# Who sums the two row halves at a group's end: ScalarE copies one half, VectorE adds the other from PSUM, and the swap is issued there

## The chip, the cores and the metric

The kernel runs on one core of a Trainium2 chip. Its time is that of the device, in microseconds (us), for one execution. Three executions were timed and one more was profiled.

## The reference

Two blocks follow each other. The first is an attention with polynomial features, and its output, turned into a matrix x of 4352 rows and 128 columns, is the input of the second. The second routes each row over eight experts with weights that are balanced by eight rounds of row and column normalisation, and adds up the experts' outputs:

```python
def _moe_ref(x, w_gate, w1, w2):
    logits = x @ w_gate
    logits = logits - logits.max()
    P = np.exp(logits)
    for _ in range(8):
        P /= P.sum(1, keepdims=True) + 1e-09
        P /= P.sum(0, keepdims=True) + 1e-09
        P *= N / E
    out = np.zeros((N, D), dtype=np.float32)
    for e in range(E):
        h = np.maximum(x @ w1[e], 0.0)
        ye = h @ w2[e]
        out += P[:, e:e + 1] * ye
    return out.astype(np.float32)
```

w1 has the shape 8 x 128 x 1024, w2 the shape 8 x 1024 x 128, all in float32.

## The kernel before

The attention, the routing weights and a part of the experts' work fill the first 197 us of the profiled execution. The rest is the function `weighted()`, in which the change lies.

**Groups, items, passes.** The rows of x are split into ten groups (`wgroups`). Groups 0 to 4 have 2 x 256 rows, groups 5 to 9 have 2 x 224 (n = 256 and n = 224). Each group goes through its list of experts; a pair of a group and an expert is an item, and each item is done in two halves of the hidden layer (s = 0 and s = 1). One half of an item is called a pass here. There are 120 of them, numbered 0 to 119 in the order of the list `todo`. Groups 1 to 8 multiply with seven products of half size in place of eight (a Strassen form); groups 0 and 9 (`whole`) use eight in the second layer.

**The order inside a pass.** Two generators take turns step by step. `firsts(t)` makes pass t's hidden layer: in each of its seven steps TensorE runs four 64 x 64 tiles in a form of two matmul records each (line 986) into the PSUM tiles `pair`, and ScalarE and VectorE turn them into h and ts (ScalarE: copies of lines 1061, 1067, 1070 and the relu of 993; VectorE: the additions of line 990, then lines 1086, 1092, 1093, 1094). `seconds(t - 1)` multiplies the pass before it with w2 (line 1120) and sums up in four PSUM banks, `acc[g][rho][q]`: rho tells the lower from the upper 64 rows of the array, q the two column halves of the result. So the last products of a group run in the first pass of the next group. That pass is called the closing pass; in the pass behind it the next group's first products are written into the same four banks, and in `into` the lower rows' products stand ahead of the upper rows' in each step. All engines take their instructions in the order in which the program issues them, which is written out by hand here.

**The end of a group.** When a bank pair q is complete, `ended(g, q)` has ScalarE copy the lower and the upper rows' sums to the tile `z` (line 1163): q = 0 in the closing pass's fourth step, q = 1 in its last (group 0 has only one pair, which is complete at the very end). The sum over rho, and for the seven-product form nine further additions, are not issued at once. They are put in the list `leisure`, and taken from it one by one at fixed places in later passes: `spare` gives them to VectorE, twice in each pass with s = 0, and `aside` to GpSimd, once in most passes. An entry None uses up a place and does nothing. The nine additions need the other 64 partitions' values, which a swap of two DMAs puts into the tile `w` (line 1192, SP's queue); it is issued along with the second sum over rho, and three entries None follow it. Then the result is added to `kept`, transposed and stored (`put`, lines 1214 and 681). `z`, `y` and `w` each exist once, so the next group's copy to z waits for the last reader of the old one.

In the last group (`LAST`) more places are taken: two at the start of its second passes and two at each `spare`. What is still left is issued on VectorE ahead of the last additions (`finish_last`, line 1235).

**SP's queue.** SP issues nearly all DMAs in the program's order: the stores; the weights of the next item, first layer at the start of a pass with s = 0 (line 851), second layer at the start of one with s = 1 (lines 860 and 862, w and ws); the routing weights (line 893); the swap of the inputs xf (line 904). Each waits in place until its buffer is free or its data is ready.

Of the kernel before, what the change touches and what calls it, by code (L numbers as in the profile page):

```python
# [10 lines left out]
F32 = mybir.dt.float32  # L11
U32 = mybir.dt.uint32
Act = mybir.ActivationFunctionType
Alu = mybir.AluOpType
# [36 lines left out]
def kernel(  # L51
# [12 lines left out]
    nc = tc.nc  # L64
    P = nc.NUM_PARTITIONS
# [887 lines left out]
    def weighted():  # L953
# [2 lines left out]
        pairs = [fps.tile([P, 2, 512], F32, name=f"pair{i}") for i in range(2)]  # L956
        copies = late[0].tile([P, 2, 3, 2 * NW], F32, name="copies", bufs=1)
        leisure, chores = [], []
        acc, counts = {}, {}
        todo = [(i, s) for i in range(len(witems)) for s in range(2)]  # L960

        def flat(t, n):
            return t.rearrange("p (r n) -> p r n", r=2)
# [6 lines left out]
        def firsts(t):  # L970
# [113 lines left out]
                relu(h[:, 3], h[:, 3])  # L1084
            else:
                nc.vector.scalar_tensor_tensor(ts[:, 0], h[:, 3], 0.0, h[:, 0], op0=Alu.max, op1=Alu.subtract)  # L1086
            spare(0)
            yield
            product(pa, 3, 7, False, True)
            relu(flat(h[:, 1], n), pa)  # L1090
            if g not in whole:
                nc.vector.tensor_tensor(ts[:, 2], h[:, 1], ts[:, 0], op=Alu.subtract)  # L1092
                nc.vector.scalar_tensor_tensor(ts[:, 1], h[:, 3], 0.0, h[:, 1], op0=Alu.max, op1=Alu.subtract)
                nc.vector.tensor_tensor(ts[:, 3], h[:, 2], ts[:, 2], op=Alu.subtract)  # L1094
            spare(1)
            yield

        def seconds(t):

            i, s = todo[t]  # L1100
            g, e = witems[i]
            lo, n, es = wgroups[g]
            _, w2, ws = forms[i]
            h, ts = rooms(t)
            if g not in acc:
                acc[g] = [[mps.tile([P, 512], F32, tag=f"s{2 * rho + q}", name="s") for q in range(2)]
                          for rho in range(2)]

            def raw(dh, k, r):
                return w2[:, 4 * r + 2 * k + s, H2 * dh:H2 * (dh + 1)]  # L1110

            def form(m, r):
                return ws[:, m, 2 * r + s]

            def into(half, w, x, r, q, place):
                per = 2 * len(es) * (4 if g == LAST else 8 if g == 0 else 3 if q else 4)
                for rho in range(2):
                    rows = slice(H2 * rho, H2 * (rho + 1))
                    c = counts[g, rho, q, half] = counts.get((g, rho, q, half), 0) + 1
                    yield lambda rho=rho, rows=rows, c=c: nc.tensor.matmul(  # L1120
                        acc[g][rho][q][H2 * half:H2 * (half + 1), n * place:n * (place + 1)], w[rows],
                        flat(x, n)[rows, r], start=c == 1, stop=c == per, tile_position=(H2 * rho, H2 * half))

            def both(x, y):
                for one, two_ in zip(x, y):
                    one()
                    two_()

            last = t + 1 == len(todo) or witems[todo[t + 1][0]][0] != g
            if g in whole:  # L1130
                for m, (k, u, b) in enumerate(((0, 0, 0), (1, 0, 2), (0, 1, 3), (1, 1, 1))):
                    for r in range(2):
                        q = u if g == LAST else 0
                        both(into(0, raw(0, k, r), h[:, b], r, q, u), into(1, raw(1, k, r), h[:, b], r, q, u))
                        if last and m == 3 and r == 1 and g == 0:
                            ended(g, 0)
                            finish_direct(g)
                        if last and m % 2 and r == 1 and g == LAST:
                            finish_last(g, u)
                        yield  # L1140
                return
            for m, (x, y) in enumerate((((raw, (0, 0), h[:, 0], 0, 0), (raw, (0, 1), h[:, 2], 0, 0)),
                                        ((form, (3,), h[:, 1], 0, 1), (form, (0,), ts[:, 0], 0, 1)),
                                        ((form, (2,), ts[:, 1], 1, 0), (form, (1,), ts[:, 2], 1, 0)))):
                for r in range(2):
                    both(into(0, x[0](*x[1], r), x[2], r, *x[3:]), into(1, y[0](*y[1], r), y[2], r, *y[3:]))
                    if last and m == 1 and r == 1:
                        ended(g, 0)
                    yield
            both(into(0, raw(1, 1, 0), ts[:, 3], 0, 1, 1), into(1, raw(1, 1, 1), ts[:, 3], 1, 1, 1))  # L1150
            if last:
                ended(g, 1)
                finish_seven(g)
            yield

        ends = {}

        def ended(g, q):
            n = wgroups[g][1]
            if g not in ends:  # L1160
                ends[g] = late[0].tile([P, 2, 2, 2 * NW], F32, tag="z", name="z", bufs=1)
            for rho in range(2):
                nc.scalar.copy(ends[g][:, rho, q, 0:2 * n], acc[g][rho][q][:, 0:2 * n])  # L1163

        def settle(g):
            while chores and chores[0][0] <= g:
# [3 lines left out]
        def plus(out_, x, y):  # L1170
            leisure.append((lambda engine: engine.tensor_tensor(out_, x, y, op=Alu.add), True))

        def finish_direct(g):
            settle(g)
            n = wgroups[g][1]
            z = ends[g]
            y = late[0].tile([P, 2, NW], F32, tag="y", name="y", bufs=1)[:, :, 0:n]
            plus(y, flat(z[:, 0, 0, 0:2 * n], n), flat(z[:, 1, 0, 0:2 * n], n))
            out_of(g, y)

        def finish_seven(g):
            settle(g)
            n = wgroups[g][1]
            z = ends[g]
            y = late[0].tile([P, 2, NW], F32, tag="y", name="y", bufs=1)[:, :, 0:n]
            w = late[0].tile([P, 2, 2 * NW], F32, tag="w", name="w", bufs=1)
            for q in range(2):
                plus(z[:, 0, q, 0:2 * n], z[:, 0, q, 0:2 * n], z[:, 1, q, 0:2 * n])

            def swap():  # L1190
                for s in range(2):
                    nc.sync.dma_start(out=w[H2 * (1 - s):H2 * (2 - s), :, 0:2 * n],
                                      in_=z[H2 * s:H2 * (s + 1), 0, :, 0:2 * n])

            last_sum = leisure.pop()[0]
            leisure.append((lambda engine: (last_sum(engine), swap()), True))
            leisure.extend([None] * 3)
            v, x = ([[u[:, q, n * a:n * (a + 1)] for a in range(2)] for q in range(2)] for u in (z[:, 0], w))
            t1, t2, t3 = (z[:, 1, 0, 0:n], z[:, 1, 0, n:2 * n], z[:, 1, 1, 0:n])
            lo_, up = lower, upper  # L1200
            plus(y[lo_, 0], v[0][0][lo_], x[0][0][lo_])
            plus(t1[lo_], v[0][0][lo_], x[1][0][lo_])
            plus(t1[up], x[0][0][up], v[1][0][up])
            plus(t2[lo_], x[0][1][lo_], v[0][1][lo_])
            plus(t1[up], t1[up], x[1][0][up])
            plus(y[lo_, 1], t1[lo_], t2[lo_])
            plus(t3[up], v[1][1][up], x[1][1][up])
            plus(y[up, 1], t1[up], v[0][1][up])
            plus(y[up, 0], t1[up], t3[up])
            out_of(g, y)  # L1210
# [154 lines left out]
```

## Time and profile before

| | |
|---|---|
| median of three runs | 916.24 us |
| lowest and highest | 915.18 and 918.57 us |
| profiled execution | 916.32 us |
| span of that execution | 914.5 us |
| mean granted clock of TensorE | 0.996 |
| busy: TensorE, VectorE, ScalarE, GpSimd | 98%, 79%, 61%, 28% |

The span runs from the first to the last instruction; the profiled execution's own time is 1.8 us longer. Busy TensorE time is modelled from pipelined matmuls, so 98% doesn't say that nothing is lost: how much a stretch loses is better read from the distance between the same step of two passes. Times in the timeline count from the start of the span. "<-" in brackets names what ended an engine's idle time before an instruction.

### The profile page before, as it was taken

Reading aid. Unit: us, or ns where it says so; the run is one execution under the profiler, and the core shown is the slowest. Engines: PE = TensorE matmul, PEld = TensorE weight load, DVE = VectorE, ACT = ScalarE, POOL = GpSimd, SP = SyncE. Lnnn points to the kernel's source line nnn. Section 1 sums busy time; section 2 is a strip of 40 time slices with the busy share of each in tenths; the row PEclk is TensorE's granted clock in tenths of the full one; section 3 lists DMA queues with packets and bytes.
Section 4 is the critical chain, followed back from the end, with each engine's and each line's share of the span. In section 5 each row is a group of like instructions: output and inputs, shape, how many; then the busy total and the mean of one; then the engine's idle time right before and its main releaser. Section 6 shows DMA issues by size and latency. Waiting matters only on the chain.

```text
span 914.5 us, 35882 instructions
## 1 busy us (share of the span) xinstructions
PE 897.1 (98%) x15484; PEld 664.8 (73%) x15484; DVE 720.3 (79%) x1261; ACT 555.6 (61%) x1109; POOL 253.8 (28%) x304
## 2 busy tenths in 40 slices
PE   9999999999999999999999999999999999999995
PEld 5777544558887667677767767777998877897884
DVE  7678699864545888888888888888898888888863
ACT  3355465546766666666666666666666666666662
POOL 3121100055552322333133213322322323333210
PEclk9999999999999999999999999999999999999998
DMA  9994100348886685577567658656865965956951
GB/s 251 310 275 166 53 1 1 76 118 277 262 261 187 195 282 178 165 249 228 153 201 241 194 155 257 231 176 182 278 208 175 293 205 169 282 185 190 282 155 37
DMA packets 124781, 177.97 MB, mean 195 GB/s; under 512 B 28976, under 2 KB 94720, under 8 KB 117584
## 3 DMA queue, kind: packets, MB, share of 16 engines
q1 hardware_dynamic: 121920, 170.18, 60.5%
q0 software_dynamic: 1600, 5.36, 2.0%
q8 instruction: 122, 2.00, 0.9%
q14 instruction: 35, 0.29, 0.1%
q10 hardware_dynamic: 1104, 0.15, 0.1%
HBM read 137.24 MB, written 19.57 MB: 171 GB/s over the span
## 4 chain that ended last, share of the span: by engine, by line
PE 88%; DVE 3%; ACT 2%; DMA 2%; issue 2%; POOL 1%; SPq 1%; DVEq 0%; ACTq 0%; POOLq 0%
PE s L1120 35%; PE pair L986 35%; PE a L711 7%; PE s L772 6%; ACT z L1163 1%; PE a L305 1%; DVE hb L990 1%; PE a L420 1%; PE a L118 1%; DMA w<-z 1%; DVE hb L726 1%; DMA w1x<-w1x 1%; ACT hb L993 1%; SPq L681 0%; DVE hb L1086 0%
## 5 line engine op out<-in xcount | busy, mean ns | idle before, releaser
L986 PE MATMUL pair<-xf,w1x 64*64 64x256 f32 (+1 forms) x6736 | 542.1, 366 | 9.3 <-DVE hb L990 5.2
L986 PEld LDWEIGHTS pair<-xf,w1x 64*64 64x64 f32 x6736 | 288.9, 133 | 88.4 <-DVE hb L990 6.3
L990 DVE TENSOR_TENSOR hb<-pair,copies 128x512 f32<-128x512 f32 (+1 forms) x354 | 234.4, 663 | 125.2 <-PE pair L986 49.8
L1120 PE MATMUL s<-hb,w 64*64 64x256 f32 (+1 forms) x3600 | 285.1, 368 | 1.0 <-ACT hb L993 0.4
L1120 PE MATMUL s<-hb,ws 64*64 64x256 f32 (+1 forms) x3264 | 263.7, 364 | 0.0
L993 ACT ACTIVATE hb<-hb 128x512 f32<-128x512 f32 (+1 forms) x252 | 153.3, 609 | 116.9 <-DVE hb L990 112.7
L1120 PEld LDWEIGHTS s<-hb,w 64*64 64x64 f32 x3600 | 159.9, 134 | 42.0 <-ACT hb L993 2.4
L1120 PEld LDWEIGHTS s<-hb,ws 64*64 64x64 f32 x3264 | 145.9, 133 | 36.7
L901 POOL TENSOR_TENSOR xf<-xT,pb 128x512 f32<-128x512 f32 (+1 forms) x60 | 74.1, 1236 | 301.0 <-ACT xf L1003 210.7
L910 POOL TENSOR_TENSOR xf<-xf 128x512 f32<-128x512 f32 (+1 forms) x52 | 63.2, 1215 | 221.7 <-ACT xf L1003 158.2
L711 PE MATMUL a<-xT,w 128*64 128x416 f32 (+3 forms) x512 | 120.9, 466 | 0.0
L713 ACT ACTIVATE hb<-a 128x416 f32<-128x416 f32 (+3 forms) x128 | 59.7, 468 | 68.0 <-PE a L711 56.7
L993 ACT ACTIVATE hb<-pair 128x512 f32<-128x512 f32 (+1 forms) x126 | 72.3, 574 | 38.3 <-PE pair L986 38.3
L1067 ACT COPY copies<-pair 128x512 f32<-128x512 f32 (+1 forms) x118 | 66.9, 567 | 30.1 <-PE pair L986 30.1
L1061 ACT COPY copies<-pair 128x512 f32<-128x512 f32 (+1 forms) x118 | 66.8, 566 | 30.1 <-PE pair L986 29.9
L1070 ACT COPY copies<-pair 128x512 f32<-128x512 f32 (+1 forms) x118 | 66.4, 563 | 30.7 <-PE pair L986 30.7
L1086 DVE SCALAR_TENSOR_TENSOR hb<-hb 128x512 f32<-128x512 f32 (+1 forms) x102 | 68.0, 667 | 11.3 <-DVE hb L990 0.9
L726 DVE TENSOR_TENSOR hb<-hb 128x416 f32<-128x416 f32 (+7 forms) x84 | 60.0, 715 | 20.8 <-ACT hb L713 15.5
L772 PE MATMUL s<-hb,ws 128*64 128x416 f32 (+3 forms) x224 | 70.9, 475 | 0.7 <-DVE hb L726 0.6
L1092 DVE TENSOR_TENSOR hb<-hb 128x512 f32<-128x512 f32 (+1 forms) x102 | 66.5, 652 | 4.3 <-ACT hb L993 2.2
L711 PEld LDWEIGHTS a<-xT,w 128*64 128x64 f32 x512 | 49.4, 137 | 25.2 <-issue 15.9
L1094 DVE TENSOR_TENSOR hb<-hb 128x512 f32<-128x512 f32 (+1 forms) x102 | 66.6, 653 | 0.0
(176 smaller groups left out, 679.8 us busy)
## 6 DMA issues: line engine op xcount, KB each, us to landing
w1x<-w1x SPq DMA_DIRECT2D x52, 1024.0 KB, 5.1
w<-in_moe_w_dram SPq DMA_DIRECT2D x56, 512.0 KB, 4.8
ws<-ws SPq DMA_DIRECT2D x52, 512.0 KB, 5.8
pb<-pT SPq DMA_DIRECT2D x35, 256.0 KB, 5.4
xf<-xf SPq DMA_DIRECT2D x70, 128.0 KB, 2.6
pb<-pT SPq DMA_DIRECT2D x25, 224.0 KB, 6.7
xf<-xf SPq DMA_DIRECT2D x50, 112.0 KB, 2.9
w1x<-in_moe_w_dram SPq DMA_DIRECT2D x28, 128.0 KB, 6.4
```

The costliest lines, as they stand in the source:

```text
L711: nc.tensor.matmul(ph[sl], loaded_w[j][0][:, P * f + H2 * s:P * f + H2 * (s + 1)], xT[:, at + lo:at + hi], start=True, stop=True, tile_pos ...
L726: nc.vector.tensor_tensor(out, a, b, op=Alu.subtract)
L772: nc.tensor.matmul(sums[g][i][H2 * s:H2 * (s + 1)], w, x, start=c == 1, stop=c == per, tile_position=(0, H2 * s))
L901: nc.gpsimd.tensor_tensor(xf[:, 0:2].rearrange("p b n -> p (b n)"), xT[:, lo:lo + 2 * n], weights.pop(i), op=Alu.mult)
L986: nc.tensor.matmul(out[H2 * col:H2 * (col + 1), r], w1[rows, form, o:o + H2], xf[rows, x], start=start, stop=stop, tile_position=(H2 * r, ...
L990: nc.vector.tensor_tensor(flat(out, n), x, flat(y, n), op=Alu.add)
L993: nc.scalar.activation(out=x, in_=y, func=Act.Relu)
L1061: nc.scalar.copy(flat(p1, n), pa)
L1067: nc.scalar.copy(flat(p5, n), pc)
L1086: nc.vector.scalar_tensor_tensor(ts[:, 0], h[:, 3], 0.0, h[:, 0], op0=Alu.max, op1=Alu.subtract)
L1094: nc.vector.tensor_tensor(ts[:, 3], h[:, 2], ts[:, 2], op=Alu.subtract)
L1120: yield lambda rho=rho, rows=rows, c=c: nc.tensor.matmul(acc[g][rho][q][H2 * half:H2 * (half + 1), n * place:n * (place + 1)], w[rows], fl ...
```

## The change

At a group's end ScalarE copies only the lower rows' sums. VectorE adds the upper rows' sums to them, reading PSUM, in a new function `add_half`. For q = 0 that add stands in the closing pass in place of `spare(0)`, behind line 1086; for q = 1 it stands at the very end of that pass; `spare(1)` is left out there. The swap's two DMAs are issued right behind the second add. The two sums over rho disappear from `leisure`; three entries None stay (five for group 8, whose last places come in the last group). The nine additions use a small tile `t` of their own for what they kept in `z`. In group 0 the add stands at the end of its last step, and z itself serves as y.

```diff
@@ firsts
-            spare(0)
+            if ending:
+                add_half(ending[0], 0)
+            else:
+                spare(0)
...
-            spare(1)
+            if not ending:
+                spare(1)
@@ seconds
                             ended(g, 0)
+                            add_half(g, 0)
                             finish_direct(g)
...
                         ended(g, 0)
+                        ending.append(g)
                     yield
...
                 ended(g, 1)
+                add_half(g, 1)
                 finish_seven(g)
+                ending.clear()
@@ ended
-                ends[g] = late[0].tile([P, 2, 2, 2 * NW], F32, tag="z", name="z", bufs=1)
-            for rho in range(2):
-                nc.scalar.copy(ends[g][:, rho, q, 0:2 * n], acc[g][rho][q][:, 0:2 * n])
+                ends[g] = late[0].tile([P, 2, 2 * NW], F32, tag="z", name="z", bufs=1)
+            nc.scalar.copy(ends[g][:, q, 0:2 * n], acc[g][0][q][:, 0:2 * n])
+
+        def add_half(g, q):
+            n = wgroups[g][1]
+            z = ends[g][:, q, 0:2 * n]
+            nc.vector.tensor_tensor(z, acc[g][1][q][:, 0:2 * n], z, op=Alu.add)
@@ finish_direct
-            z = ends[g]
-            y = late[0].tile([P, 2, NW], F32, tag="y", name="y", bufs=1)[:, :, 0:n]
-            plus(y, flat(z[:, 0, 0, 0:2 * n], n), flat(z[:, 1, 0, 0:2 * n], n))
-            out_of(g, y)
+            out_of(g, flat(ends[g][:, 0, 0:2 * n], n))
@@ finish_seven
-            for q in range(2):
-                plus(z[:, 0, q, 0:2 * n], z[:, 0, q, 0:2 * n], z[:, 1, q, 0:2 * n])
-
-            def swap():
-                for s in range(2):
-                    nc.sync.dma_start(out=w[H2 * (1 - s):H2 * (2 - s), :, 0:2 * n],
-                                      in_=z[H2 * s:H2 * (s + 1), 0, :, 0:2 * n])
-
-            last_sum = leisure.pop()[0]
-            leisure.append((lambda engine: (last_sum(engine), swap()), True))
-            leisure.extend([None] * 3)
...
+            t = late[0].tile([P, 3, NW], F32, tag="t", name="t", bufs=1)
+            for s in range(2):
+                nc.sync.dma_start(out=w[H2 * (1 - s):H2 * (2 - s), :, 0:2 * n], in_=z[H2 * s:H2 * (s + 1), :, 0:2 * n])
+            leisure.extend([None] * (5 if g + 1 == LAST else 3))
```

More of the change, by code (lines that the diff above doesn't have):

```diff
@@ L958, in weighted @@
         leisure, chores = [], []
-        acc, counts = {}, {}
+        acc, counts, ending = {}, {}, []
         todo = [(i, s) for i in range(len(witems)) for s in range(2)]
@@ L1186, in finish_seven @@
             w = late[0].tile([P, 2, 2 * NW], F32, tag="w", name="w", bufs=1)
-            for q in range(2):
-                plus(z[:, 0, q, 0:2 * n], z[:, 0, q, 0:2 * n], z[:, 1, q, 0:2 * n])
-            def swap():
-                for s in range(2):
-                    nc.sync.dma_start(out=w[H2 * (1 - s):H2 * (2 - s), :, 0:2 * n],
-                                      in_=z[H2 * s:H2 * (s + 1), 0, :, 0:2 * n])
-            last_sum = leisure.pop()[0]
-            leisure.append((lambda engine: (last_sum(engine), swap()), True))
-            leisure.extend([None] * 3)
-            v, x = ([[u[:, q, n * a:n * (a + 1)] for a in range(2)] for q in range(2)] for u in (z[:, 0], w))
-            t1, t2, t3 = (z[:, 1, 0, 0:n], z[:, 1, 0, n:2 * n], z[:, 1, 1, 0:n])
+            t = late[0].tile([P, 3, NW], F32, tag="t", name="t", bufs=1)
+            for s in range(2):
+                nc.sync.dma_start(out=w[H2 * (1 - s):H2 * (2 - s), :, 0:2 * n], in_=z[H2 * s:H2 * (s + 1), :, 0:2 * n])
+            leisure.extend([None] * (5 if g + 1 == LAST else 3))
+            v, x = ([[u[:, q, n * a:n * (a + 1)] for a in range(2)] for q in range(2)] for u in (z, w))
+            t1, t2, t3 = (t[:, a, 0:n] for a in range(3))
             lo_, up = lower, upper
```

## The prediction

> **What bounds the kernel now.** I read the page first, then what TensorE waits for, then its stretches, then the timeline around the longest waits.
>
> ```profile
> PE 897.1 (98%) x15484; PEld 664.8 (73%) x15484; DVE 720.3 (79%) x1261; ACT 555.6 (61%) x1109; POOL 253.8 (28%) x304
> ```
>
> TensorE is the bound, so only what shortens its waits counts; ScalarE's 61% says that fewer copies are worth nothing as work. The view of waits, TensorE alone:
>
> ```profile
> PE pair L986 <- DVE hb L990: 5.2, 1, 5.2
> PE pair L986 <- ACT copies L1061: 2.2, 8, 0.3
> ```
>
> One wait of 5.2 us, and eight behind ScalarE's copies. The weighted stage is 120 passes, each beginning with its first L986 matmul; the windows view, cut there, gives a pass's length in column two (later columns: busy time of PE, PEld, DVE, ACT, POOL, then granted clock).
>
> ```profile
> 289.15:295.96 6.81, 6.58 (x116) 4.51 (x112) 4.07 (x8) 4.19 (x9) 1.28 (x1) 1.00 0.90 246
> 302.00:308.04 6.04, 6.04 (x116) 4.17 (x114) 5.31 (x9) 3.80 (x8) 2.10 (x3) 1.00 0.73 216
> 374.52:381.19 6.67, 6.47 (x118) 4.45 (x116) 4.84 (x8) 4.96 (x11) 1.97 (x2) 1.00 0.84 227
> 459.76:466.26 6.50, 6.28 (x117) 4.17 (x113) 4.67 (x8) 4.79 (x11) 1.97 (x2) 1.00 0.71 220
> 544.82:551.32 6.50, 6.28 (x117) 4.18 (x113) 4.66 (x8) 4.79 (x11) 1.95 (x2) 1.00 0.70 193
> 629.51:635.35 5.84, 5.52 (x117) 4.16 (x112) 4.32 (x9) 4.40 (x11) 1.14 (x1) 1.00 0.60 142
> 693.76:699.69 5.93, 5.64 (x117) 4.27 (x116) 4.85 (x10) 4.48 (x11) 1.76 (x2) 1.00 0.55 115
> 699.69:704.99 5.30, 5.30 (x116) 4.27 (x112) 4.71 (x10) 3.49 (x8) 1.14 (x1) 1.00 0.98 376
> 758.79:765.48 6.69, 6.17 (x117) 4.24 (x113) 4.82 (x10) 5.25 (x13) 1.77 (x2) 1.00 0.28 55
> 824.50:831.20 6.70, 6.17 (x119) 4.26 (x113) 4.83 (x10) 5.26 (x13) 1.76 (x2) 1.00 0.27 53
> 847.09:853.65 6.56, 5.70 (x116) 4.73 (x109) 4.97 (x10) 3.89 (x8) 1.76 (x2) 1.00 1.03 274
> 853.65:859.43 5.78, 5.75 (x112) 5.10 (x116) 3.83 (x8) 2.99 (x7) 1.75 (x2) 1.00 0.92 342
> 880.72:887.41 6.69, 6.16 (x126) 4.43 (x121) 4.36 (x10) 5.34 (x13) 1.15 (x1) 1.00 0.25 38
> 887.41:900.34 12.93, 7.74 (x124) 5.43 (x120) 4.45 (x12) 4.22 (x8) 0.65 (x1) 0.78 0.43 118
> 900.34:914.55 14.21, 9.43 (x188) 6.75 (x180) 4.64 (x11) 3.76 (x7) 0.66 (x1) 0.96 0.12 17
> ```
>
> An undisturbed pass takes 6.04 us (n = 256, row 302.00) or 5.30 us (n = 224, row 699.69). Nine rows are the passes that follow a group's closing pass (289.15 to 693.76 without 302.00; 758.79, 824.50, 880.72): over their undisturbed length by 0.77, 0.63, 0.46, 0.46, 0.54, 0.63, 1.39, 1.40 and 1.39, together 7.7 us. Rows 847.09 and 853.65 lose 1.74, and row 887.41 loses 7.63. That is all the change can reach.
>
> **Part one: the swap.** Group 8's swap today, on SP's queue, and what waited for it on VectorE:
>
> ```profile
> 880.81 5.62 SPq L681 DMA_DIRECT2D out_dram<-yt  x12
> 886.53 1.17 SPq L860 DMA_DIRECT2D w<-in_moe_w_dram  x1
> 887.74 0.58 SPq L862 DMA_DIRECT2D ws<-ws  x1
> 888.42 1.30 SPq L1192 DMA_DIRECT2D w<-z  x2
> ```
> ```profile
> 882.74 0.62 DVE L1171 TENSOR_TENSOR z<-z 128x448 f32<-128x448 f32 x1 [0.74 <-ACT z L1163]
> ```
> ```profile
> 895.28 0.38 DVE L1171 TENSOR_TENSOR y<-z,w 64x224 f32<-64x224 f32 x1 [7.79 <-DMA w<-z]
> ```
>
> The sums were ready at 883.36, but the swap's instructions stood behind twelve stores and two weight loads, were issued at 888.42, and landed just before 895.28. VectorE takes its queue in order, so the next pass's h additions (L990) waited behind the first use of w, and TensorE behind them. In the changed order the two adds run at the end of the closing pass and the swap is SP's next instruction, at about 883, ahead of both loads. The stores now come later, because with two leisure places fewer the previous group's last items are taken one pass later. Followed place by place, with five empty places, the first use of w moves to the end of pass 118 (row 887.41), some 9 us after the issue; the old swap took 6.9. The wait goes: 12.93 becomes 5.30, **-7.63**.
>
> The blocks after the wait ran at half rate:
>
> ```profile
> 900.34 0.97 PE L986 MATMUL pair<-xf,w1x 64*64 64x224 f32 x8
> 901.09 0.74 PE L1120 MATMUL s<-hb,w 64*64 64x224 f32 x8
> 901.66 0.36 PE L986 MATMUL pair<-xf,w1x 64*64 64x224 f32 x4
> ```
>
> Two blocks of eight take 1.32 us here (900.34 to 901.66), against 5.30/14 = 0.38 each: another **-0.56** in the last stretch. Three sums that were done early are now drained on VectorE before the last additions; they lie beside TensorE's last products but may push the store by 0 to 0.6: **+0.2**.
>
> **Part two: the group ends.** Removed are 17 ScalarE copies; added are 17 VectorE adds that read PSUM; 17 leisure sums go (some on GpSimd, which has 28% busy and bounds nothing). The nearest rows for an add:
>
> ```profile
> L990 DVE TENSOR_TENSOR hb<-pair,copies 128x512 f32<-128x512 f32 x204 | 141.0, 691 | 93.2 <-PE pair L986 43.4 <-ACT xf L1003 22.8 <-ACT ws L1003 16.9
> L990 DVE TENSOR_TENSOR hb<-pair,copies 128x448 f32<-128x448 f32 x150 | 93.4, 624 | 32.0 <-ACT xf L1003 16.3 <-PE pair L986 6.4
> ```
>
> So 0.69 or 0.62 us. The Trainium skill speaks against this exchange: its page "VectorE: DVE Perf Modes", under Specifications, places VectorE closer to SBUF and ScalarE closer to PSUM. By that sentence alone the adds would come out dearer. The trace's rows above already are adds with one operand in PSUM, so their 0.69 and 0.62 hold whatever that distance costs.
>
> What ScalarE's shorter queue gives back, VectorE takes elsewhere. The next group's first products (L1120) write the same banks: the lower rows' bank is free when ScalarE has copied it, but the upper rows' bank now waits for VectorE's add, which stands behind L1086 of the closing pass.
>
> ```profile
> 374.45 0.69 DVE L1086 SCALAR_TENSOR_TENSOR hb<-hb 128x512 f32<-128x512 f32 x1
> ```
> ```profile
> 374.95 0.38 PE L1120 MATMUL s<-hb,w 64*64 64x256 f32 x1
> ```
>
> The add ends at 374.45 + 0.69 + 0.69 less some 0.08 of overlap, 375.75. TensorE's first L1120 block starts at 374.95 and reaches the upper rows half a block (0.22) later, 375.17. New wait 0.6: the pass is 6.64, against 6.67, 6.50 and 6.50 now: -0.03 + 0.14 + 0.14; row 629.51 I leave at 0. For n = 224:
>
> ```profile
> 693.69 0.63 DVE L1086 SCALAR_TENSOR_TENSOR hb<-hb 128x448 f32<-128x448 f32 x1
> ```
>
> 693.69 + 0.63 + 0.62 - 0.08 = 694.86, against 693.76 + 0.38 + 0.19 = 694.33: 0.55, a pass of 5.85, so -0.08 at row 693.76. In the passes ahead of rows 758.79 and 824.50 ScalarE's copy also waited for GpSimd's last leisure sum on the old z:
>
> ```profile
> 758.42 0.97 ACT L1163 COPY z<-s 128x448 f32<-128x448 f32 x2 [0.73 <-POOL y L1171]
> ```
>
> With one queue place fewer that wait goes at the first of them; at the second it stays, but one copy fewer stands behind it. Both come down to 5.85: -0.84 and -0.85. Group 9 has no L1086, so its add is in time; row 880.72 loses the two copies (0.97) from ScalarE's queue, 6.69 to 5.72: -0.97.
>
> Group 0 ends differently: both copies come with the pass's last products, and TensorE already waits for the second.
>
> ```profile
> 290.49 0.68 DVE L1094 TENSOR_TENSOR hb<-hb 128x512 f32<-128x512 f32 x1
> ```
> ```profile
> 290.02 0.92 PE L1120 MATMUL s<-hb,w 64*64 64x256 f32 x6 [0.23 <-ACT z L1163]
> ```
>
> In VectorE's order the add stands behind L1094: 290.49 + 0.68 + 0.69 - 0.08, so TensorE resumes at about 291.85 where undisturbed it would be at 289.15 + 0.43 + 0.22 = 289.80. A wait of 2.05, the pass 8.09 for 6.81: **+1.28**, the change's clear loss. Together the nine give **-1.2**.
>
> **Part three: queues.** SP now holds from the closing pass's end until the second add is done, and behind it stand the next weights (L860, L862) and, a pass later, L851 and the xf swaps. Worked out for the end at 693.76: behind L1086 (693.69) come the first add, three operations and the second add, 0.6 each with their overlap, so it is done at 697.3; two swap issues take 1.3 (row 888.42); L860 goes at 698.6, L862 0.6 later. Two passes on, at 704.99, TensorE needs w and some 1.5 later ws: 6.4 and 7.3 us of room; for n = 256 about 1.5 more. How long w (L860) and ws (L862) take today, by their tiles' views:
>
> ```profile
> DMA to landing us min/median/max: 4.2/4.8/7.5
> ```
> ```profile
> DMA to landing us min/median/max: 5.0/6.0/8.3
> ```
>
> At the medians nothing is late; at the maxima about 1.1 us at each of three n = 224 ends. I take 0, the side of the medians; bound +3.3. On the other side, the loss in rows 847.09 and 853.65 I read as mostly a late w1x:
>
> ```profile
> 836.49:841.79 5.30, 5.30 (x116) 4.27 (x112) 4.93 (x10) 3.49 (x8) 2.24 (x2) 1.00 0.85 270
> ```
> ```profile
> 843.12 0.75 SPq L851 DMA_DIRECT2D w1x<-w1x  x1
> ```
>
> It was issued 1.3 us into the pass that begins at 841.79, right behind group 7's swap, for the pass that begins at 853.65. That swap goes out two passes earlier now. Bounds 0 and -1.74; I take **-1.0**, since other traffic stays.
>
> **Sum:** -7.63 - 0.56 + 0.2 - 1.2 - 1.0 = -10.2 us. The profiled execution took 916.32 us (span 914.5 and 1.8 around it), 0.08 above the runs' median. 916.3 - 10.2 = **906.1 us**. A measurement of this kernel can tell about 0.5%, 4.6 us, from no change. Main case: 903.9 (the whole 1.74 back, the waits 0.2 shorter) to 910.4 (none of the 1.0 back, all 3.3 of late weights).
>
> **Rivals.**
> *The swap stays late* (0.08). If SP's queue or the DMA traffic still lands w after its first use, 8.2 us stay: 914.3, no change. For it: landings of 6 to 8 us under load; against: 9 us of room.
>
> *The group ends heal* (0.06). If TensorE does not reach the upper rows' bank before the add, the nine waits of 7.7 all but vanish instead of giving 1.2: 899.9. Against it stands the order in VectorE's queue above.
>
> *The 2 us wait halves the clock* (0.07). Row 887.41 has a granted clock of 0.78 after 5.2 idle us, and half rate for some 5 us, to 901.66, costing about 2.5. No idle of 2 us is in this stage to show what it does. If it does the same: 908.6. The Trainium skill's "TensorE: Matmul & The Clock Gate", Part 1, has the clock fall only after an idle window of about 3.4 us; the drop after 5.2 agrees, and by that rule this rival fails.
>
> *Slower: the held SP queue starves TensorE* (0.06). Every group end with a swap now puts swap, w2, ws and w1x into SP's queue within some 4 us. If the weights land 9 us after their issue instead of 5 to 6, TensorE stands about 2.5 us at each of eight ends: 906.1 + 20 = 926. It decides from 1.85 each (14.8 in all, the gain of 10.2 and 4.6 more). Against it:
>
> ```profile
> 829.95 1.63 SPq L860 DMA_DIRECT2D w<-in_moe_w_dram  x1
> ```
>
> Issued 5.5 us into the pass at 824.50, later than I expect of any, these weights still left the pass two later (row 836.49) at 5.30.
>
> *Main case* 0.73.
>
> **How the numbers follow.** The range 903.0 to 910.5 holds the main case and the clock's; left out are 0.08 + 0.06 + 0.06. Faster by over 0.5% (under 911.7): 0.73 + 0.07 + 0.06 = 0.86; same 0.08; slower 0.06.
>
> **What would show it.** Right: L1192 issued before L860 at each end; no wait of VectorE on w<-z; pass 118 at 5.3 with clock 1.00; TensorE's waits at L1120 behind VectorE's new add, 0.6 each, 2 at the first; none behind L1061. Wrong: waits of L1120 or L986 on w, ws or w1x two passes after an end, or a clock below 1.00 after 292.

## The result, and the profile after

The changed kernel took 910.15 us (median of five runs, 909.9 to 911.91), the kernel before 916.64 us (five runs): a ratio of 0.9926, with a 95% interval of 0.9901 to 0.995. It is faster, by a little under 1%; the time lies inside the forecast range and 4 us short of the forecast. The profiled execution took 910.05 us (span 908.3), 6.3 less than the one before, where the sum had said 10.2.

The busy times of the engines, from the page:

```profile
PE 895.1 (99%) x15484; PEld 703.5 (77%) x15484; DVE 721.9 (79%) x1268; ACT 548.9 (60%) x1092; POOL 245.2 (27%) x297
```

The 17 ScalarE copies fewer (1109 to 1092 instructions) and the VectorE adds more hardly move a total. What moved is in the windows, cut at each pass's first L986 matmul (after the busy times come TensorE's granted clock, the share of the DMA engines and their GB/s). In order these are passes 15, 29, 43, 57, 71, 83, 88, 95, 107, 111, 112, 117, 118 and the last stretch:

```profile
291.01:299.14 8.13, 6.74 (x114) 4.49 (x110) 4.67 (x9) 3.70 (x8) 1.28 (x1) 1.00 0.66 212
377.71:384.52 6.81, 6.47 (x118) 5.10 (x115) 5.78 (x10) 4.19 (x9) 1.97 (x2) 1.00 0.61 136
463.08:469.89 6.81, 6.47 (x117) 5.14 (x115) 5.78 (x10) 4.19 (x9) 1.97 (x2) 1.00 0.57 139
548.80:555.43 6.63, 6.47 (x116) 5.13 (x111) 5.60 (x10) 4.01 (x9) 1.90 (x2) 1.00 0.55 130
633.62:639.74 6.12, 5.75 (x118) 5.16 (x114) 5.28 (x10) 3.90 (x9) 1.76 (x2) 1.00 0.58 140
698.18:704.25 6.07, 5.86 (x120) 5.32 (x116) 5.17 (x10) 3.81 (x9) 1.76 (x2) 1.00 0.40 85
725.71:732.30 6.59, 5.62 (x119) 4.64 (x116) 4.79 (x10) 3.57 (x8) 1.75 (x2) 1.00 0.84 296
764.08:770.07 5.99, 5.76 (x117) 5.14 (x112) 5.09 (x10) 3.73 (x9) 1.76 (x2) 1.00 0.42 90
828.75:834.82 6.07, 6.07 (x119) 5.38 (x116) 5.26 (x10) 4.47 (x11) 1.81 (x2) 1.00 0.37 77
850.71:856.01 5.30, 5.30 (x119) 5.25 (x116) 4.41 (x9) 3.49 (x8) 1.15 (x1) 1.00 0.59 164
856.01:861.31 5.30, 5.30 (x119) 5.25 (x117) 4.71 (x10) 3.49 (x8) 1.15 (x1) 1.00 1.02 358
882.49:888.48 5.99, 5.99 (x126) 4.57 (x124) 4.28 (x10) 4.64 (x11) 1.15 (x1) 1.00 0.39 91
888.48:894.15 5.67, 5.67 (x124) 4.58 (x120) 3.36 (x9) 3.75 (x8) 0.66 (x1) 1.00 0.78 208
894.15:908.30 14.15, 8.89 (x188) 6.87 (x180) 7.02 (x17) 4.17 (x8) 0.00 (x0) 0.98 0.14 22
```

Pass 118 is down from 12.93 to 5.67, passes 111 and 112 from 6.56 and 5.78 to 5.30 each. Pass 15 is up from 6.81 to 8.13, and the other eight group ends are mixed. In SP's part of the timeline group 8's swap (L1198, formerly L1192) now stands ahead of both weight loads and the twelve stores (the last row merges these with the last group's four). In VectorE's part the first use of w comes 8.9 us after the issue and waits for nothing. GpSimd, which takes another of the nine additions, came for w earlier and began at 888.95, when the swap had landed; no engine waited for that addition:

```profile
884.50 1.30 SPq L1198 DMA_DIRECT2D w<-z  x2
885.89 0.55 SPq L860 DMA_DIRECT2D w<-in_moe_w_dram  x1
886.54 1.02 SPq L862 DMA_DIRECT2D ws<-ws  x1
888.49 17.18 SPq L681 DMA_DIRECT2D out_dram<-yt  x16
```
```profile
893.43 0.37 DVE L1183 TENSOR_TENSOR y<-z,w 64x224 f32<-64x224 f32 x1
```
```profile
888.95 0.66 POOL L1183 TENSOR_TENSOR t<-w,z 64x224 f32<-64x224 f32 x1 [1.91 <-DMA w<-z]
```

TensorE's waits (engine, line, what it waited for: total, times, longest) show the new one, at seven places, and only one for second-layer weights. That one lies at 213.72, in pass 3, ahead of the first group's end:

```profile
PE s L1124 <- DVE z L1175: 2.8, 7, 1.2
PE s L1124 <- DMA w<-in_moe_w_dram: 0.4, 1, 0.4
```

How the new wait arises at the second group end, from VectorE's and TensorE's parts of the timeline:

```profile
377.64 0.69 DVE L1086 SCALAR_TENSOR_TENSOR hb<-hb 128x512 f32<-128x512 f32 x1
378.25 0.68 DVE L1175 TENSOR_TENSOR z<-s,z 128x512 f32<-128x512 f32 x1
378.85 0.68 DVE L1095 TENSOR_TENSOR hb<-hb 128x512 f32<-128x512 f32 x1
```
```profile
379.08 0.43 PE L1124 MATMUL s<-hb,w 64*64 64x256 f32 x2 [0.34 <-DVE z L1175]
```

The add (L1175) queues behind L1086, as forecast, and ends at 378.25 + 0.68 = 378.93. TensorE writes the bank that the add has read only at 379.08, 0.15 behind its end. In pass 15 the same add stands behind three others (L1095 to L1097) and TensorE, after a wait of 0.23 us, waits 1.17 us in one piece:

```profile
292.96 0.69 DVE L1175 TENSOR_TENSOR z<-s,z 128x512 f32<-128x512 f32 x1
```
```profile
293.70 0.43 PE L1124 MATMUL s<-hb,w 64*64 64x256 f32 x2 [1.17 <-DVE z L1175]
```

### The profile page after: what moved, and what is told of

It reads as the page before. It is cut to its first block, busy times and chain, and to the rows that moved or that the text cites. A ratio compares the mean times of both kernels' runs of the same rounds, so it can differ in the third digit from the quotient of the medians.

```text
span 908.3 us, 35879 instructions
## 1 busy us (share of the span) xinstructions
PE 895.1 (99%) x15484; PEld 703.5 (77%) x15484; DVE 721.9 (79%) x1268; ACT 548.9 (60%) x1092; POOL 245.2 (27%) x297
## 4 chain that ended last, share of the span: by engine, by line
PE 84%; issue 10%; DVE 2%; POOL 1%; DMA 1%; ACT 1%; SPq 0%; POOLq 0%; DVEq 0%; ACTq 0%
PE s L1124 37%; PE pair L986 36%; PE a L711 4%; PE s L772 3%; PE a L305 1%; PE a L118 1%; PE a L420 1%; DMA w<-in_moe_w_dram 1%; DVE hb L990 1%; DVE hb L1086 1%; DVE z L1175 0%; PE a L272 0%; DMA pb<-pT 0%; PE s L334 0%; POOL xf L901 0%
## 5 line engine op out<-in xcount | busy, mean ns | idle before, releaser
L986 PE MATMUL pair<-xf,w1x 64*64 64x256 f32 (+1 forms) x6736 | 603.4, 366 | 2.0 <-ACT xf L1003 1.0
L986 PEld LDWEIGHTS pair<-xf,w1x 64*64 64x64 f32 x6736 | 337.8, 133 | 55.7 <-ACT hb L993 1.9
L1124 PE MATMUL s<-hb,w 64*64 64x256 f32 (+1 forms) x3600 | 312.4, 366 | 3.4 <-DVE z L1175 2.8
L1124 PE MATMUL s<-hb,ws 64*64 64x256 f32 (+1 forms) x3264 | 300.6, 364 | 0.0
L1124 PEld LDWEIGHTS s<-hb,w 64*64 64x64 f32 x3600 | 185.0, 133 | 38.7 <-PE pair L986 4.0
L1124 PEld LDWEIGHTS s<-hb,ws 64*64 64x64 f32 x3264 | 180.7, 133 | 27.7
L1086 DVE SCALAR_TENSOR_TENSOR hb<-hb 128x512 f32<-128x512 f32 (+1 forms) x102 | 67.8, 665 | 10.6
L1095 DVE TENSOR_TENSOR hb<-hb 128x512 f32<-128x512 f32 (+1 forms) x102 | 66.5, 652 | 1.7
L1097 DVE TENSOR_TENSOR hb<-hb 128x512 f32<-128x512 f32 (+1 forms) x102 | 66.8, 655 | 0.0
```

The costliest lines, as they stand in the source:

```text
L986: nc.tensor.matmul(out[H2 * col:H2 * (col + 1), r], w1[rows, form, o:o + H2], xf[rows, x], start=start, stop=stop, tile_position=(H2 * r, ...
L1124: yield lambda rho=rho, rows=rows, c=c: nc.tensor.matmul(acc[g][rho][q][H2 * half:H2 * (half + 1), n * place:n * (place + 1)], w[rows], fl ...
```

## The experiments

The main theory: the gain comes from the early swap alone (issued at the group's end, first used later); that VectorE now reads the upper rows from PSUM costs a little at the ends, because the add stands too late in VectorE's queue. The rivals: the gain comes from fewer ScalarE copies; or the ends are dearer because reading PSUM is slow on VectorE; or the missing 4 us are weights that come late. All edits are to the changed kernel. The first four kernels (after_again among them) ran together on one chip, the other four together on another.

This table sums up the ten profiles: stretches in us, cut at the same matmuls everywhere. "Ends" is the sum of the nine passes behind a closing pass (15, 29, 43, 57, 71, 83, 95, 107, 117).

| | start of pass 0 | ends | 87+88 | 111+112 | 118 | last stretch | span |
|---|---|---|---|---|---|---|---|
| before | 192.6 | 58.3 | 11.0 | 12.3 | 12.9 | 14.2 | 914.5 |
| before_again | 193.8 | 58.3 | 11.0 | 13.7 | 13.2 | 13.8 | 916.0 |
| after | 194.2 | 58.6 | 12.2 | 10.6 | 5.7 | 14.1 | 908.3 |
| after_again | 193.2 | 58.4 | 12.4 | 10.6 | 5.7 | 14.2 | 907.8 |
| e1_swap_early | 193.7 | 57.7 | 11.0 | 10.6 | 5.7 | 13.6 | 905.6 |
| e2_swap_late | 193.7 | 58.6 | 17.6 | 10.6 | 5.7 | 19.4 | 924.9 |
| e3_add_ahead | 193.4 | 54.2 | 13.1 | 10.8 | 5.7 | 13.6 | 904.1 |
| e5_both | 194.0 | 52.7 | 12.7 | 10.7 | 5.7 | 13.6 | 903.0 |
| e6_rest | 193.4 | 51.9 | 12.2 | 10.6 | 5.7 | 13.7 | 901.7 |
| e7_no_load_45 | 194.7 | 58.6 | 13.3 | 10.6 | 5.7 | 14.7 | 910.7 |

**The changed kernel again** (no edit).

> The changed kernel, unaltered, profiled a second time. The first profile of it gained 6.3 us on the one of before, but 1.9 us of that had been lost by 213 us of the span, ahead of the first group's end, where both programs issue the same work. Theory (that loss is scatter between executions): the start of the first pass moves by a us or so again, to somewhere between 191.5 and 195.5 us, while the nine passes behind the group ends come back within 0.1 us (8.13, 6.81, 6.81, 6.63, 6.12, 6.07, 5.99, 6.07, 5.99), and the single stall of 1.3 us in the pass at 725.7 does not come back at that place. Rival (the change itself costs 2 us early on, through other placement of tiles): the start of the first pass is at 194.2 again within 0.3.

909.82 us (909.32 to 911.43), ratio 0.9924 (0.9906 to 0.9942). It repeats, and so do the nine ends, to 0.25 us in the sum. Pass 0 begins 1.0 us earlier than in the first profile, at 193.2. The stall in pass 88, which I had expected to be gone, came back: 6.87 us.

**The swap alone.** ScalarE copies both halves again, the lower ones to z, the upper ones to a tile of their own; VectorE adds them from SBUF at the same two places, and the swap is issued there.

```diff
-            nc.scalar.copy(ends[g][:, q, 0:2 * n], acc[g][0][q][:, 0:2 * n])
...
+            for rho, z in enumerate((ends[g], uppers[g])):
+                nc.scalar.copy(z[:, q, 0:2 * n], acc[g][rho][q][:, 0:2 * n])
...
-            nc.vector.tensor_tensor(z, acc[g][1][q][:, 0:2 * n], z, op=Alu.add)
+            nc.vector.tensor_tensor(z, uppers[g][:, q, 0:2 * n], z, op=Alu.add)
```

> The swap's part alone: ScalarE copies both row halves as in the kernel before, and VectorE adds them at the same places as in the changed kernel, but from SBUF; the swap is issued there too. Theory (the gain is the swap's, and the reading of PSUM by VectorE gives about nothing in sum): pass 118 at 5.3 to 5.7 us and the passes 111 and 112 at 5.30, as in the changed kernel; the pass behind group 0's end back at 6.81, the n = 256 ends at 6.5 to 6.7, the n = 224 ends at 5.9 to 6.7; in all within 1.5 us of the changed kernel, 908 to 911. Rival (the gain comes from ScalarE's relief): 914 to 917 us, as before.

907.72 us (907.09 to 908.91), ratio 0.9899 (0.988 to 0.9918), 2.1 us less than the changed kernel beside it. So the whole gain is there with all of ScalarE's copies still in place. Fewer copies are out as its cause; what this version keeps is the early swap and the later first use of w, and no run has the early issue with the old first use. An estimate from the rows of group 8: in the changed kernel w had landed by 888.95. A first use at the place that it had in the kernel before, 0.08 us into the pass (887.49 against 887.41), would have come at 888.56 and waited some 0.4 us. With the old issue, 1.01 us into pass 118, and the old 6.9 us to the first use, w would have come at about 896.3, 2.9 us too late even for the later use at 893.43. So the issue weighs more than the later use. The windows of passes 29, 107 and the last stretch, and the view of waits:

```profile
376.08:382.76 6.68, 6.47 (x119) 4.45 (x116) 5.96 (x10) 4.98 (x11) 1.97 (x2) 1.00 0.57 144
824.51:831.30 6.79, 6.18 (x118) 4.29 (x116) 5.45 (x10) 5.35 (x13) 1.81 (x2) 1.00 0.38 82
891.96:905.60 13.64, 8.88 (x188) 6.87 (x180) 7.01 (x17) 4.17 (x8) 0.00 (x0) 0.96 0.14 20
```
```profile
PE pair L986 <- ACT copies L1061: 2.2, 8, 0.3
```

These ends are those of before (6.67 and 6.70 there), with the same eight waits behind ScalarE's copies, 2.2 us; only pass 95 is shorter, 5.93 for 6.69. With the copies split between two engines these waits went, and others of the same size came. That is so only while the add stands behind L1086: without pass 15 the other eight ends are 51.5 us in the kernel before, 50.9 here and 46.1 in e3 below, where VectorE reads PSUM one place earlier. Leaving copies out does pay there.

**The swap later.** It becomes an entry of `leisure`, one place behind the group's first empty place, with as many places in all as in the changed kernel.

```diff
-            for s in range(2):
-                nc.sync.dma_start(...)
-            leisure.extend([None] * (5 if g + 1 == LAST else 3))
+            def swap():
+                for s in range(2):
+                    nc.sync.dma_start(...)
+
+            leisure.append(None)
+            leisure.append((lambda engine: swap(), True))
+            leisure.extend([None] * (3 if g + 1 == LAST else 1))
```

> The changed kernel with the swap's two DMAs issued one leisure place later than the group's first empty place, as late as in the kernel before, in place of at the group's end; the number of places is the same. Theory (the early issue is what took the wait of 5.2 us away): for group 8 the swap is issued behind the stores of group 7's results, at about 893 to 897 us, VectorE waits for w at the end of pass 118, and the two last passes lose 1 to 5 us with some matmuls at half rate if TensorE stands over 3 us; 911 to 917 us. Rival (the wait went because fewer leisure places were needed, not because of the issue): no wait on w, 909 to 911 us.

928.06 us (922.18 to 931.76), ratio 1.0114 (1.0078 to 1.015): slower than the kernel before, where 911 to 917 had been expected. The expectation had followed group 8 alone. VectorE's and TensorE's waits:

```profile
DVE y L1183 <- DMA w<-z: 16.3, 4, 5.9
```
```profile
PE pair L986 <- DVE hb L990: 12.6, 4, 4.9
```

Four groups, not one, now use w before it has landed. The windows of passes 87, 101 and 113 and of the last stretch show them:

```profile
720.36:732.13 11.77, 6.83 (x118) 5.60 (x116) 5.25 (x10) 3.85 (x8) 1.75 (x2) 0.90 0.82 225
802.18:811.67 9.49, 7.10 (x119) 5.71 (x117) 5.25 (x10) 3.83 (x8) 1.13 (x1) 0.82 0.80 221
870.62:878.10 7.48, 5.78 (x118) 4.73 (x116) 5.63 (x10) 3.53 (x8) 2.64 (x2) 1.00 1.06 317
905.57:924.95 19.38, 10.80 (x188) 7.77 (x180) 8.17 (x19) 4.17 (x8) 0.86 (x1) 0.89 0.18 38
```

The empty places are what covers the swap's flight. With one behind the swap, three with the last group, they don't; with all of them behind it, as in the changed kernel, VectorE never waits for w. So the swap's place counts, at four ends. But this issue is later than the one of the kernel before, since the closing pass has no leisure places any more: group 8's goes out at 906.56, 1.0 us into pass 119, where it was 1.0 us into pass 118. What the old place would have cost with the later first use is told by the estimate above alone.

**The add ahead of L1086.** If the new waits come from the add's place in VectorE's queue, they go when it moves one instruction forward; if VectorE is slow at PSUM, they stay.

```diff
+            if ending:
+                add_half(ending[0], 0)
             if g in whole:
...
-            if ending:
-                add_half(ending[0], 0)
-            else:
+            if not ending:
                 spare(0)
```

> The changed kernel with the first add of each group 1 to 8 issued ahead of line 1086 in place of behind it. Theory (the passes behind the ends lose 0.6 to 0.8 us because TensorE's first product on the upper rows' bank waits for that add, which stands behind 1086): the add ends 0.6 us earlier, 0.1 us after TensorE wants the bank; the six passes at 6.81, 6.81, 6.63, 6.12, 6.07 and 6.07 come down to 6.2, 6.2, 6.2, 5.5, 5.45 and 5.45, the one of group 6 likewise from 5.99; 3.5 to 4.5 us less in all, 905 to 907. Group 0's and group 8's ends stay at 8.13 and 5.99. Rival (the wait is set by ScalarE's copy or by the adding itself, not by the place): the passes stay within 0.2 us, 909 to 911. A second rival: line 1086 and what follows it come late instead and hold TensorE as long as before.

906.30 us (904.89 to 908.46), ratio 0.9885 (0.9864 to 0.9906), 3.5 less than the changed kernel beside it. Windows of passes 29, 83, 88 and 107, then VectorE at pass 28's end:

```profile
376.86:382.91 6.05, 6.05 (x119) 4.38 (x116) 5.58 (x10) 4.20 (x9) 1.97 (x2) 1.00 0.52 128
694.13:699.43 5.30, 5.30 (x117) 5.12 (x112) 4.93 (x10) 3.77 (x9) 1.77 (x2) 1.00 0.35 75
721.46:728.48 7.02, 5.62 (x119) 4.63 (x115) 4.79 (x10) 3.57 (x8) 1.75 (x2) 1.00 0.92 318
823.82:829.71 5.89, 5.89 (x118) 5.35 (x114) 5.28 (x10) 4.47 (x11) 1.81 (x2) 1.00 0.31 70
```
```profile
376.59 0.68 DVE L1175 TENSOR_TENSOR z<-s,z 128x512 f32<-128x512 f32 x1
377.19 0.68 DVE L1088 SCALAR_TENSOR_TENSOR hb<-hb 128x512 f32<-128x512 f32 x1
```

The add takes the same 0.68 us, ends 0.4 after the pass's first matmul (376.86) instead of 1.2 after it (377.71 in the changed kernel), and passes 29 and 83 are undisturbed: 6.05 and 5.30. I had expected 6.2 and 5.45; the whole wait went. It was the place in the queue. Passes 87 and 88 lost more than in the changed kernel (pass 88, row 721.46: 7.02 for 6.59): the last experiment looks there. Pass 107 stays at 5.89 for another reason, in ScalarE's timeline:

```profile
823.50 0.53 ACT L1170 COPY z<-s 128x448 f32<-128x448 f32 x1 [0.73 <-POOL y L1183]
```

The copy to z waits for GpSimd's last reader of the group before, as it did in the kernel before.

**And group 0.** As e3, and in group 0 ScalarE copies both halves again, the upper ones to a tile of their own, and the sum is taken from `leisure`.

```diff
-                            add_half(g, 0)
+                            upper0[g] = late[0].tile([P, 2 * NW], F32, tag="u0", name="upper0", bufs=1)[:, 0:2 * n]
+                            nc.scalar.copy(upper0[g], acc[g][1][0][:, 0:2 * n])
...
-            out_of(g, flat(ends[g][:, 0, 0:2 * n], n))
+            plus(z, z, upper0[g])
+            out_of(g, flat(z, n))
```

> The changed kernel with the add ahead of line 1086 (as in the run before it) and, for group 0, both copies left to ScalarE and the sum left to the leisure list, as in the kernel before. Theory (in group 0 the add stands behind three operations of VectorE and holds TensorE for 2 us, the second copy for 0.8): the pass behind group 0's end 6.81 in place of 8.11, all others as in the run with the add ahead; 1.3 us less than it, 905.0. Rival (TensorE waits there for the first copy anyway): 8.1 again and 906.3.

905.99 us (903.17 to 906.64) beside a kernel before of 918.39 on this chip: ratio 0.9863 (0.984 to 0.9887). Pass 15 is back at its length of before:

```profile
290.81:297.60 6.79, 6.55 (x116) 4.47 (x112) 4.05 (x8) 4.19 (x9) 1.28 (x1) 1.00 0.83 245
```

**The two ends that were left.** As e5, with z twice (`bufs=2`), and in group 8's closing pass the relu of h's fourth quarter by VectorE in place of ScalarE.

```diff
-                ends[g] = late[0].tile([P, 2, 2 * NW], F32, tag="z", name="z", bufs=1)
+                ends[g] = late[0].tile([P, 2, 2 * NW], F32, tag="z", name="z", bufs=2)
...
             if g in whole:
-                relu(h[:, 3], h[:, 3])
+                if ending:
+                    nc.vector.tensor_scalar_max(h[:, 3], h[:, 3], 0.0)
+                else:
+                    relu(h[:, 3], h[:, 3])
```

> The version before it with two buffers for z, and with the relu of h3 in group 8's closing pass on VectorE in place of ScalarE. Theory (at group 6's end ScalarE's copy waits 0.7 us for GpSimd's last reader of the old z; at group 8's end ScalarE's queue is 0.6 us too long): the pass behind group 6's end 5.30 in place of 5.89, the one behind group 8's end 5.4 in place of 5.99, 1.2 us less in all, 903.8. Rival (both waits come from elsewhere, say from DMAs that stand in SP's queue): no change against the version before it.

904.95 us (903.53 to 906.1), ratio 0.9861 (0.9836 to 0.9885), the best of all; that it beats e5 by 1.0 lies within the two intervals, but its passes 107 and 117 show the step:

```profile
822.11:827.44 5.33, 5.33 (x119) 5.19 (x114) 4.96 (x10) 3.80 (x9) 1.79 (x2) 1.00 0.34 77
876.62:882.33 5.71, 5.71 (x127) 5.66 (x124) 4.48 (x11) 4.28 (x10) 1.15 (x1) 1.00 0.42 97
```

Pass 107 came down from 5.89 to 5.33, as expected; pass 117 from 5.99 to 5.71, not to the 5.4 expected.

**The kernel before again** (no edit), to see how far the part ahead of the change scatters.

> The kernel before, unaltered, profiled a second time. Its first profile began the first pass at 192.6 us; the five profiles of changed kernels so far, whose instructions up to there are the same, at 193.2 to 194.2. Theory (scatter): it begins somewhere in 192.5 to 194.5, likely above 193. Rival (something before the weighted stage is really later in the changed kernels): 192.6 within 0.2. The passes behind the ends come back within 0.1 us of the first profile (6.81, 6.67, 6.50, 6.50, 5.84, 5.93, 6.69, 6.70, 6.69), pass 118 at 12.9 within 1; pass 88 again at about 5.65.

917.8 us (one run, span 916.0). Pass 0 begins at 193.79, against 192.62 in the first profile: the same instructions, 1.2 us apart. Over all ten profiles it begins between 192.6 and 194.7. Eight of the nine ends come back to 0.01 us, pass 83 is 0.08 shorter. Passes 111 and 112 do not come back: 13.7 us for 12.3.

**A load less at the stall in pass 88.** In the changed kernel TensorE stands still there, with a releaser (ScalarE's L1003) that had ended at 728.74:

```profile
729.23 0.61 PE L986 MATMUL pair<-xf,w1x 64*64 64x224 f32 x8 [0.97 <-ACT xf L1003]
```

In the changed kernel's two profiles TensorE went on 1.2 and 1.3 us behind the end of a 16 KB transfer on the queue that carries most of the instructions, and first-layer weights were landing at the time. The theory: the weights' transfer holds that fetch up. This kernel leaves the load of item 45's weights out, so that item is computed with the weights of the expert before it.

```diff
-        if same(i):
+        if same(i) or i == 45:
```

> The changed kernel with the weights of item 45 not loaded: that item uses those of item 44 (its part of the output is computed with another expert's weights). That takes away the 1 MB transfer issued at the start of pass 88 and 1 MB more in pass 89. In the changed kernel pass 88 took 6.6 to 6.9 us in two profiles, with TensorE standing 1.0 to 1.2 us right behind the end of a 16 KB transfer of the queue that carries instructions. Theory (TensorE runs out of instructions because that fetch is held up by the weights' transfers): pass 88 at 5.3 to 5.5. Rival (the fetch's place or something in the pass itself is the cause): pass 88 again at 6.4 to 7.0, or the stall at the same count of instructions.

912.48 us (one run). Windows of passes 87 and 88:

```profile
720.78:727.99 7.21, 5.59 (x118) 5.15 (x116) 4.48 (x9) 3.48 (x8) 1.76 (x2) 1.00 1.08 327
727.99:734.04 6.05, 5.63 (x120) 4.64 (x117) 4.80 (x10) 3.58 (x8) 1.75 (x2) 1.00 0.21 63
```

Traffic in pass 88 fell (from 296 to 63 GB/s), and it is 0.5 shorter, but a gap of 1.62 us came in pass 87 and the two together are 13.3 us, more than the 12.2 of the changed kernel. So the load of item 45 does not make the gap. The instruction transfers themselves are not ruled out: from pass 15 on, the ten profiles have 13 gaps of over 0.4 us in which the named releaser, if any, had ended over 0.4 us before TensorE went on, in passes 87, 88 and 111 to 113. In all 13 TensorE goes on 1.2 to 1.7 us behind the end of such a transfer. But each profile has 94 of these transfers from pass 15 on, and most leave no gap (the first profile of before and e1 have none at all of that size). What makes them stays open.

## Why the prediction was right, and where it was off

The direction, the swap's mechanism and the range held; the sum was 4.0 too large, worked out here term by term against the first profile of before (span -6.2). That the time stayed inside the range, 0.35 us from its upper end, is in part luck: the room above 906.1 was put there for weights that come late, which they did not, and other losses used it up, ahead of pass 15, in passes 87 and 88 and at the ends.

| term | forecast | measured |
|---|---|---|
| pass 118 | -7.63 | -7.26 |
| last stretch | -0.36 | -0.06 |
| the nine ends | -1.2 | +0.29 |
| passes 111 and 112 | -1.0 | -1.74 |
| ahead of pass 15 | 0 | +1.86 |
| all other passes | 0 | +0.7 |

*Part one, the swap: right.* Issue at 884.50, 2.01 us into pass 117 (forecast about 883, 2.3 us into it as it lay in the first profile of before); VectorE's first use at the end of pass 118, 8.9 us later, no wait. The mis-sized bit is the undisturbed length of pass 118: I took 5.30, it is 5.67. Group 9 uses eight products in its second layer, so `seconds` issues one block more there, 0.378 by the forecast's own figure.

*The last stretch.* The two terms of its -0.36 come apart here. The last pair of additions before and after, with the last transpose after it in the changed kernel, from VectorE's part of the timeline:

```profile
909.82 0.89 DVE L1235 TENSOR_TENSOR kept<-s,kept 128x224 f32<-128x224 f32 x2
```
```profile
903.07 0.89 DVE L1237 TENSOR_TENSOR kept<-s,kept 128x224 f32<-128x224 f32 x2
904.35 0.41 DVE L1216 STREAM_TRANSPOSE yt<-kept 128x224 f32<-128x224 f32 x1 [0.39 <-DVE kept L1237]
```

The last pair starts 9.48 us into the stretch before and 8.92 after: the -0.56 came as forecast (in the second profile of before, where less of the stretch ran at half rate, it starts at 9.11). The three drained sums do not push it. But from there to the end it takes 5.2 us for 4.7, where I had +0.2, and 0.39 of that is the pause ahead of the last transpose. The changed kernel has it both times, e7 too; e1, e3, e5 and e6 don't, with the same work there, and have 13.6 to 13.7 us. Why was not found.

*Part two, the ends: the mechanism right, the size wrong.* The clear loss, pass 15, was forecast at +1.28 and is +1.32. At the others the add stands and ends where the forecast had put it (378.93 is 1.22 into pass 29; forecast 375.75, 1.23 in), but TensorE goes on 0.15 behind it, at all six ends that have the wait besides pass 15 (0.05 there), a step that the forecast had left out. The 0.6 and 0.55 over the undisturbed length became 0.59 to 0.82. Five more ends came out dearer than before, by 0.13 to 0.31, where the forecast had -0.08 to +0.14; the two with -0.84 and -0.85 came to -0.70 and -0.63; group 9's -0.97 came to -0.70. The runs showed it from the other side: with the add one place earlier the ends fall by 4.2 us (e3), with VectorE's add from SBUF they are those of before (e1). Two sums of the forecast are slightly off as written: 290.49 + 0.68 + 0.69 - 0.08 is 291.78, not 291.85, and 694.86 - 694.33 is 0.53, not 0.55; neither changes the account.

*Part three, the queues: right for the weights, and the rest came on top.* The whole 1.74 came back where I took 1.0. L851, which stood 1.33 us into pass 110 in the kernel before, is issued at that pass's start. That w1x was late there can be read from the kernel before itself, from the view of L851 at 843.12 and TensorE's weight loads:

```profile
DMA to landing us min/median/max: 10.4/10.4/10.4
```
```profile
853.62 0.24 PEld L986 LDWEIGHTS pair<-xf,w1x 64*64 64x64 f32 x8 [0.97 <-DVE hb L1086]
```

It landed at 853.5, and pass 112's first weight load, which reads it, began at 853.62 after 0.97 us of standing still; L1086, the name beside it, had ended at 853.33. So about 1.0 of the 1.74 was the late w1x, the forecast's very figure. The other 0.7 has no cause here. In the second profile of before the two passes lose 3.05 us, nearly all in two of the unexplained gaps (1.43 and 0.99), and w1x arrives in time. The second-layer weights were not late at any end: bound +3.3, measured 0. That the missing time was late weights is out.

*Ahead of pass 15.* The first profile of before was the fastest of all ten up to pass 0. Against the second one (span 916.0) the change gives -7.7, not -6.2. This is no step of the argument that failed, but the reference of the sum; two profiles of before would have shown it.

*All other passes.* Passes 87 and 88 alone took 1.2 more. e1 and both profiles of before have 11.0 there, the other versions 12.2 and more; in e2 that is mostly the wait for w, in the others the cause is open (above).

*The rivals.* The swap did not stay late. The ends did not heal by themselves, though e3 shows that one instruction's place was all that was missing. The clock did not halve: pass 15 has a granted clock of 1.00. But its wait came as 0.23 and 1.17 us, never as 2 us in one piece, so this does not test the rival. The kernel with the later swap (e2) does: a wait of 1.70 us in pass 113 left the clock at 1.00 (row 870.62), while one of 2.39 us in pass 101 (clock 0.82, row 802.18) was followed by blocks of eight at 0.74 us from start to start, where 0.38 is usual:

```profile
808.65 1.02 PE L986 MATMUL pair<-xf,w1x 64*64 64x224 f32 x8 [2.39 <-DVE hb L990]
809.45 0.97 PE L1124 MATMUL s<-hb,ws 64*64 64x224 f32 x8
810.19 0.97 PE L986 MATMUL pair<-xf,w1x 64*64 64x224 f32 x8
```

A wait of the forecast 2.05 us lies between the two, so the rival is not refuted, and my reason against it was wrong. By the Trainium skill ("TensorE: Matmul & The Clock Gate", Part 1) the clock falls after an idle window of some 3.4 us; here 2.39 us was enough (2.79 for the weight loads), and the measurement decides. The expectation for e2, half rate if TensorE stands over 3 us, falls with it. The starved queue did not come: the passes two behind each swap that need the new weights took 6.04, or 5.30 to 5.43 for n = 224. But e2 showed a slower case that I had not listed: the same swap a little too late, at four ends at once.

*The sentence against the exchange.* The Trainium skill's page "VectorE: DVE Perf Modes", Specifications, has VectorE closer to SBUF. The view of the new line gives the add 683 ns as its median over both sizes; at 128x512 it took 0.68 us, and additions with both operands in SBUF at the same place (L1095) took 0.68 too. Over the whole stage the medians are 685 ns for both. No dearer PSUM operand shows in this kernel.

## What to carry to other kernels

When the evacuation of an accumulator moves to another engine, the bank comes free when that engine's queue gets to it: look at what stands ahead of it there, and put it in front of work that nobody waits for (one place was worth 3.5 us here). A transfer between two steps is worth issuing as soon as its data exists, ahead of loads in the same queue; how many steps lie between issue and first use has to be counted for every group, not for the last alone. And a sum of small terms should be set against more than one profile of the kernel before: up to 2 us of difference lay in work that the change doesn't touch.

## What I had not expected of the hardware

TensorE resumed 0.15 us after the end of the VectorE instruction that it waited for at six ends (378.93 to 379.08 at one of them), and 0.05 us after it in pass 15. A wait of 2.39 us was enough to bring TensorE down to half rate for 3 us (808.65 to 811.67 in e2), where one of 1.70 us was not. And it stood still for 0.5 to 1.6 us in passes 87, 88 and 111 to 113 with no releaser that ended at that time, each time 1.2 to 1.7 us behind the end of a 16 KB instruction transfer; the gaps shift with small changes of the program, and no run here found their cause.
